# Scaling the second chunk's attention probabilities on GpSimd instead of VectorE

## The chip, the cores and the metric

The kernel runs on one core of one Trainium2 chip. The metric is the device time of one execution in microseconds (us). Beside it there is one profiled execution, whose trace holds the start and the end of every instruction on every engine: TensorE (PE, with its weight loads listed apart as PEld), VectorE (DVE), ScalarE (ACT), GpSimd (POOL) and SyncE (SP).

## The reference

The work is an attention with a sparse mask, followed by a two-layer network with a GELU. Batch 4, 8 heads, 768 positions, head size 64; each position sees a window of local keys behind it and a few global keys at the start of the sequence, with a linear bias per head:

```python
scores = scale * q @ k.T + bias                # bias = -slope[h] * distance
scores = np.where(is_global | is_local, scores, -1e9)
a = np.exp(scores - max(scores)); a = a / (sum(a) + 1e-9)
x = (a @ v)                                    # heads side by side: 3072 tokens x 512
h = x @ w_in                                   # 512 x 2048
out = 0.5 * h * (1 + erf(h / sqrt(2))) @ w_out # 2048 x 512
```

The weights arrive as 64-bit words, and the kernel rebuilds each of them as a high part and a low part so that float32 accuracy survives the matmuls.

## The kernel before

The 3072 tokens are cut into 12 chunks of 256 (c = 0 to 11). For each chunk the attention is made in four pairs of heads (p = 0 to 3), and for each pair the steps are: `scores_pair` (s, L342: 16 small matmuls; then n, L353: VectorE adds the mask penalty, writes the scores to SBUF as tile `n` and keeps their minimum), `exps` (L374: four ScalarE exponentials over 128x192 elements with their sums in `su`; L376 and L377: VectorE adds 1e-9 and takes the reciprocal; L383: four instructions multiply the four pieces of `n` by the reciprocal), `flip` once per head (t, L393: three TensorE transposes; pt, L397: ScalarE copies them to SBUF), and `av_pair` (L422: the products with v; L445 and L450: ScalarE writes the high part of `x`, L174: VectorE the low part).

A chunk's tokens then go through the network in eight steps (s = 0 to 7), one for each slice of 256 hidden columns. `m1` (h, L481 in chunks 0 and 1, L464 and L468 later) is the first product, `gelu` (L491, L492 on ScalarE, L174 gl on VectorE) the activation, and `m2` (acc, L511) the second product. Chunks 0 and 1 take their steps in turn, (0,0), (1,0), (0,1), (1,1) and so on, so that each slice of weights, once rebuilt, serves both; from chunk 2 on the chunks follow one another.

While chunks 0 and 1 run, the weights are also rebuilt, four pieces for each slice: L206 (ScalarE, low words), L212, L214 and L216 (VectorE, bit operations), L226 (ScalarE, high part), L174 winl or woutl (VectorE, low part).

The loop in `run` writes all this out step by step (T), and `START` and `EVENTS` say at which T a chunk's pair gets its scores, transposes and products: chunk 1 makes its scores at T = -3, -2, -1 and 0, and its transposes two steps later. The order in which the instructions then stand on each engine's queue is made at compile time by a scheduler with a model of their durations; it is fixed when the kernel runs, and each engine takes its instructions in that order. Some orders are forced by hand: `after` and `behind` put an instruction behind another one on its engine. `behind` uses `self.last_dve`, the last of VectorE's instructions for the attention or the network that was written out, so that a piece of weights (L212, L174) never goes ahead of it.

Of the kernel before, what the change touches and what calls it, by code (L numbers as in the profile page):

```python
# [83 lines left out]
class Fast:  # L84
# [282 lines left out]
    def exps(self, c, p):  # L367
        nc = self.nc
        first = c % CPB == 0
        mn, su = self.stat.pop((c, p))  # L370
        every = [(self.pt_n[c, 2 * p + hh][:, j * NK:j * NK + (P if first and j == 0 else NK)], 2 * hh + j)
                 for hh in range(2) for j in range(2)]
        for nn, i in every:
            self.table(nc.scalar.activation(out=nn, in_=nn, func=AF.Exp, bias=mn[:, i:i + 1],  # L374
                                            scale=-1.0, accum_out=su[:, i:i + 1]))
        nc.vector.tensor_scalar(out=su, in0=su, scalar1=1e-9, scalar2=None, op0=ALU.add)  # L376
        nc.vector.reciprocal(out=su, in_=su)  # L377
        if c >= 3:
            top = self.nmax[:, 3 * NP]
            nc.vector.tensor_tensor(out=top, in0=top, in1=mn, op=ALU.max)  # L380
        for nn, i in every:
            eng = nc.vector if c < 2 else nc.gpsimd
            ins = eng.tensor_scalar(out=nn, in0=nn, scalar1=su[:, i:i + 1], scalar2=0.0,  # L383
                                    op0=ALU.mult, op1=ALU.add)
        if c < 2:
            self.last_dve = ins.ins

    def flip(self, c, h):
# [401 lines left out]
```

## Time and profile before

| | |
|---|---|
| time before, median of 3 runs | 688.21 us (687.5 to 688.92) |
| the profiled execution: its own time | 687.72 us |
| the profiled execution: span of the core | 685.9 us |
| what lies around the span | 1.82 us |
| TensorE busy | 673.2 us, 98% of the span |
| VectorE, ScalarE, GpSimd busy | 382.3, 353.9 and 103.3 us |

The span runs from the first to the last instruction of the trace. An engine's busy time is the union of its instructions, and where an engine stood idle, the trace says which instruction of another engine ended that idle time. Times in the rows below count from the start of the span.

### The profile page before, as it was taken

The page shows a single profiled execution, that of the slowest core. Times are in us where ns is not written, and L with a number is a line of the kernel's source. Part 1 is how long each engine was busy: PE and PEld are TensorE (multiplying, and loading weights), DVE is VectorE, ACT ScalarE, POOL GpSimd, SP SyncE. Part 2 cuts the span into 40 slices and gives each one's busy share as a digit, 9 for nine tenths or more (in the row PEclk, how much of TensorE's full clock was granted, in tenths as well). Part 3 has the DMA queues.
Part 4 walks back from the last instruction along what each step waited for, and adds up shares of the span by engine and source line. Part 5 has one row for each costly group of instructions (what it writes and reads, how often), then busy time and mean ns, then how long its engine had stood idle before and what let it go on. Part 6 is the DMA issues. An engine that isn't in the chain of part 4 may idle for free.

```text
span 685.9 us, 12867 instructions
## 1 busy us (share of the span) xinstructions
PE 673.2 (98%) x4879; PEld 562.0 (82%) x4879; DVE 382.3 (56%) x1129; ACT 353.9 (52%) x846; POOL 103.3 (15%) x232
## 2 busy tenths in 40 slices
PE   8989999999999999999999999999999999999996
PEld 5668988878888888888888888888888888888785
DVE  5989998334554654644545545546445455453532
ACT  3897686554654545545527536445446365362222
POOL 3100331310200301301201111031021031010000
PEclk9999999999999999999999999999999999999999
DMA  9936933240622513403314234134053152000000
GB/s 269 285 130 193 300 131 124 78 138 33 162 62 93 162 43 113 139 19 121 99 64 155 70 94 154 33 107 131 10 162 117 38 162 62 32 1 1 33 0 35
DMA packets 66037, 71.17 MB, mean 104 GB/s; under 512 B 32688, under 2 KB 49072, under 8 KB 65968
## 3 DMA queue, kind: packets, MB, share of 16 engines
q1 hardware_dynamic: 61520, 62.80, 30.5%
q10 hardware_dynamic: 4448, 7.48, 3.1%
q8 instruction: 41, 0.67, 0.4%
q14 instruction: 28, 0.23, 0.1%
HBM read 63.97 MB, written 6.29 MB: 102 GB/s over the span
## 4 chain that ended last, share of the span: by engine, by line
PE 90%; ACT 4%; DVE 3%; issue 1%; DMA 1%; ACTq 0%; DVEq 0%; SPq 0%
PE acc L511 37%; PE h L464 22%; PE h L468 8%; PE av L422 6%; PE s L342 5%; PE h L481 4%; PE t L393 4%; PE h L470 3%; PE warm_ps L361 1%; ACT n L374 1%; ACT w L206 1%; DVE n L353 1%; DVE wb L214 1%; DVE n L383 1%; DMA w<-w 1%
## 5 line engine op out<-in xcount | busy, mean ns | idle before, releaser
L464 PE MATMUL h<-x,winh 128*128 128x512 f32 x640 | 216.0, 401 | 0.0
L472 DVE TENSOR_REDUCE hs<-h 128x256 f32<-128x512 f32 x160 | 110.3, 689 | 132.6 <-PE h L470 132.0
L511 PE MATMUL acc<-wouth,gh 128*128 128x512 f32 x384 | 157.0, 409 | 1.1 <-ACT gh L491 0.8
L511 PE MATMUL acc<-woutl,gh 128*128 128x512 f32 x384 | 150.2, 391 | 0.0
L511 PE MATMUL acc<-wouth,gl 128*128 128x512 f32 x384 | 148.5, 393 | 0.0
L383 POOL TENSOR_SCALAR n<-n,su 128x192 f32<-128x192 f32 (+1 forms) x160 | 72.6, 473 | 442.0 <-ACT n L374 225.7
L468 PE MATMUL h<-x,winl 128*128 128x256 f32 x480 | 134.7, 281 | 0.0
L464 PEld LDWEIGHTS h<-x,winh 128*128 128x128 f32 x640 | 114.3, 188 | 20.4 <-issue 0.3
L174 DVE TENSOR_TENSOR gl<-gr,gh 128x512 fp32r<-128x512 f32 x96 | 66.9, 697 | 112.5 <-ACT gr L492 112.4
L491 ACT ACTIVATE gh<-hs 128x512 fp32r<-128x512 f32 x80 | 50.7, 633 | 133.2 <-DVE hs L472 129.7
L397 ACT COPY pt<-t 128x384 f32<-128x384 f32 x96 | 45.6, 480 | 133.6 <-PE t L393 133.2
L468 PEld LDWEIGHTS h<-x,winl 128*128 128x128 f32 x480 | 90.4, 188 | 7.1
L511 PEld LDWEIGHTS acc<-wouth,gh 128*128 128x128 f32 x384 | 72.2, 188 | 19.9 <-issue 5.8
L511 PEld LDWEIGHTS acc<-wouth,gl 128*128 128x128 f32 x384 | 72.1, 188 | 16.7 <-issue 0.6
L511 PEld LDWEIGHTS acc<-woutl,gh 128*128 128x128 f32 x384 | 72.3, 188 | 12.6 <-issue 0.3
L374 ACT ACTIVATE n<-n,mn 128x192 f32<-128x192 f32 (+1 forms) x144 | 62.3, 434 | 1.7 <-DVE mn L353 1.5
L353 DVE CUSTOM_DVE_ANT_0 n<-s,pen 128x192 f32<-128x192 f32 (+1 forms) x192 | 54.9, 342 | 3.5 <-PE s L342 3.5
L481 PE MATMUL h<-x,winh 128*128 128x256 f32 x256 | 49.0, 287 | 0.4 <-ACT x L445 0.2
L492 ACT ACTIVATE gr<-hs 128x512 f32<-128x512 f32 x80 | 49.3, 616 | 0.0
L393 PE MATMUL t<-ident,n 128*128 128x128 f32 x288 | 47.2, 274 | 1.2 <-DVE n L383 1.2
L422 PE MATMUL av<-pt,vr 64*64 64x64 f32 (+1 forms) x1024 | 45.5, 246 | 2.7 <-ACT pt L397 2.6
L422 PEld LDWEIGHTS av<-pt,vr 64*64 64x64 f32 (+1 forms) x1024 | 35.1, 135 | 13.1 <-issue 5.6
(81 smaller groups left out, 729.5 us busy)
## 6 DMA issues: line engine op xcount, KB each, us to landing
w<-w SPq DMA_DIRECT2D x32, 512.0 KB, 5.3
c<-w SPq DMA_DIRECT2D x32, 512.0 KB, 5.0
out<-o ACTq DMA_DIRECT2D x24, 256.0 KB, 2.0
qr<-qT SPq DMA_DIRECT2D x11, 512.0 KB, 3.8
vr<-v SPq DMA_DIRECT2D x22, 256.0 KB, 4.1
kr<-kT SPq DMA_DIRECT2D x16, 320.0 KB, 4.9
vr<-v SPq DMA_DIRECT2D x19, 192.0 KB, 3.0
kr<-kT SPq DMA_DIRECT2D x36, 64.0 KB, 3.7
```

Of the source, the lines that this page charges most:

```text
L174: return self.nc.vector.tensor_tensor(out=out, in0=in_, in1=hi.bitcast(F32), op=ALU.subtract)
L353: ins = nc.vector.tensor_tensor_reduce(out=nn[:, j * NK:j * NK + n], in0=sp[hh][:, j, 0:n], in1=pen, scale=-slope(2 * p + hh), scalar=3e38 ...
L374: self.table(nc.scalar.activation(out=nn, in_=nn, func=AF.Exp, bias=mn[:, i:i + 1], scale=-1.0, accum_out=su[:, i:i + 1]))
L383: ins = eng.tensor_scalar(out=nn, in0=nn, scalar1=su[:, i:i + 1], scalar2=0.0, op0=ALU.mult, op1=ALU.add)
L393: nc.tensor.transpose(tp[:, i, :], nn[:, o:o + P], self.ident)
L422: ins = nc.tensor.matmul(out, lhsT=lhs, rhs=rhs, start=start, stop=stop, skip_group_check=True).ins
L464: nc.tensor.matmul(hp.rearrange("p e t -> p (e t)"), lhsT=wh[:, d, fs], rhs=x[:, d].rearrange("p e t -> p (e t)"), start=d == 0, stop=d == ...
L468: nc.tensor.matmul(hp[:, 0, :], lhsT=wl[:, d - 1, fs], rhs=x[:, d - 1, 0, :], start=False, stop=False, skip_group_check=True)
L472: self.last_dve = nc.vector.tensor_reduce(out=self.h[t][:, f, :], in_=hp.rearrange("p e t -> p t e"), axis=mybir.AxisListType.X, op=ALU.ad ...
L481: nc.tensor.matmul(hp[:, f, :], lhsT=w[:, d, fs], rhs=x[:, d, e, :], start=n == 0, stop=n == 3 * NP - 1)
L491: self.table(nc.scalar.activation(out=gh, in_=hp, func=AF.Gelu))
L511: nc.tensor.matmul(acc, lhsT=g[:, f, ks], rhs=w[:, f, :], start=s == 0 and n == 0, stop=s == NST - 1 and n == 5)
```

## The change

The multiplication of the probabilities by the reciprocal of their sum (L383) is done by VectorE for chunks 0 and 1 and by GpSimd for chunks 2 to 11. Now it is done by VectorE for chunk 0 alone. Chunk 1 has four pairs with four instructions each, so 16 instructions of 128x192 float32 change their engine. The second line of the diff goes with it: `last_dve` is no longer set to chunk 1's multiplications, so the pieces of weights that follow in the program are put behind VectorE's instruction before that.

```diff
         for nn, i in every:
-            eng = nc.vector if c < 2 else nc.gpsimd
+            eng = nc.vector if c < 1 else nc.gpsimd
             ins = eng.tensor_scalar(out=nn, in0=nn, scalar1=su[:, i:i + 1], scalar2=0.0,
                                     op0=ALU.mult, op1=ALU.add)
-        if c < 2:
+        if c < 1:
             self.last_dve = ins.ins
```

## Rows read from the trace of the kernel before

**Rows 1.** Stretches of the span: start and end in us, their length, then busy time of each engine (with its number of instructions), granted TensorE clock, DMA share, GB/s. The order of the engines is PE, PEld, DVE, ACT, POOL.

```profile
24.00:40.00 16.00, 14.17 (x140) 9.96 (x138) 15.74 (x60) 14.47 (x40) 0.00 (x0) 1.00 0.82 278
40.00:50.00 10.00, 8.22 (x86) 5.36 (x85) 8.14 (x31) 9.69 (x31) 0.00 (x0) 1.00 0.34 103
50.00:60.00 10.00, 9.10 (x93) 7.78 (x92) 9.98 (x20) 6.95 (x14) 0.00 (x0) 1.00 0.49 162
60.00:70.00 10.00, 10.00 (x66) 9.07 (x65) 10.00 (x19) 6.64 (x13) 0.00 (x0) 1.00 0.68 213
134.00:300.00 166.00, 166.00 (x1214) 140.11 (x1213) 81.75 (x252) 83.57 (x201) 25.43 (x60) 1.00 0.32 98
```

**Rows 2.** Whom TensorE waited for, over the whole span: us in total, times, longest us.

```profile
PE av L422 <- ACT pt L397: 2.6, 3, 1.3
PE t L393 <- DVE n L383: 1.2, 1, 1.2
PE acc L511 <- ACT gh L491: 0.8, 1, 0.8
```

**Rows 3.** VectorE's instructions in order of time around the multiplications of chunk 1: start us, us, engine, line, operation, tiles, shapes, count, idle time before.

```profile
29.90 0.17 DVE L377 RECIPROCAL su<-su 128x4 f32<-128x4 f32 x1
...
34.98 0.17 DVE L377 RECIPROCAL su<-su 128x4 f32<-128x4 f32 x1
...
42.28 0.18 DVE L377 RECIPROCAL su<-su 128x4 f32<-128x4 f32 x1
...
43.76 0.35 DVE L353 CUSTOM_DVE_ANT_0 n<-s,pen 128x192 f32<-128x192 f32 x1
...
44.87 0.69 DVE L174 TENSOR_TENSOR winl<-wb,winh 128x512 fp32r<-128x512 f32 x1
...
46.19 0.69 DVE L216 CUSTOM_DVE_ANT_0 wb<-w,wb 128x1024 uint16<-128x1024 uint16 x1
46.80 0.17 DVE L377 RECIPROCAL su<-su 128x4 f32<-128x4 f32 x1
47.00 1.01 DVE L383 TENSOR_SCALAR n<-n,su 128x192 f32<-128x192 f32 x4
47.92 0.42 DVE L174 TENSOR_TENSOR x<-av,x 128x256 fp32r<-128x256 f32 x1
48.26 0.76 DVE L212 TENSOR_SCALAR wb<-w 128x512 int32<-128x512 int32 x2
48.93 0.42 DVE L174 TENSOR_TENSOR x<-av,x 128x256 fp32r<-128x256 f32 x1
49.26 0.69 DVE L174 TENSOR_TENSOR winl<-wb,winh 128x512 fp32r<-128x512 f32 x1
```

**Rows 4.** TensorE's instructions in order of time: chunk 1's transposes of pairs 0, 1, 2 and 3 and what follows them; same columns.

```profile
33.37 0.82 PE L393 MATMUL t<-ident,n 128*128 128x128 f32 x6
...
37.38 0.82 PE L393 MATMUL t<-ident,n 128*128 128x128 f32 x6
...
44.04 0.55 PE L393 MATMUL t<-ident,n 128*128 128x128 f32 x3
...
45.72 0.55 PE L393 MATMUL t<-ident,n 128*128 128x128 f32 x3
47.47 0.76 PE L393 MATMUL t<-ident,n 128*128 128x128 f32 x4 [1.20 <-DVE n L383]
...
48.52 0.44 PE L393 MATMUL t<-ident,n 128*128 128x128 f32 x2
49.54 0.65 PE L422 MATMUL av<-pt,vr 128*64 128x128 f32 x6 [0.58 <-ACT pt L397]
50.12 0.51 PE L481 MATMUL h<-x,winh 128*128 128x256 f32 x2
...
53.07 0.43 PE L422 MATMUL av<-pt,vr 128*64 128x128 f32 x2
```

**Rows 5.** ScalarE's instructions in order of time before and behind pair 3's exponentials; same columns.

```profile
32.28 0.46 ACT L374 ACTIVATE n<-n,nmax 128x192 f32<-128x192 f32 x1 [0.91 <-DVE nmax L353]
...
44.15 0.46 ACT L374 ACTIVATE n<-n,nmax 128x192 f32<-128x192 f32 x1 [0.29 <-DVE nmax L353]
...
49.02 0.47 ACT L397 COPY pt<-t 128x384 f32<-128x384 f32 x1
...
49.96 0.86 ACT L397 COPY pt<-t 128x384 f32<-128x384 f32 x2
```

**Rows 6.** GpSimd's instructions in order of time, same columns, and one of VectorE's beside them.

```profile
96.34 9.24 POOL L383 TENSOR_SCALAR n<-n,su 128x192 f32<-128x192 f32 x8 [18.81 <-DVE su L377]
123.62 1.63 POOL L383 TENSOR_SCALAR n<-n,su 128x192 f32<-128x192 f32 x4 [18.04 <-DVE su L377]
...
123.65 0.35 DVE L353 CUSTOM_DVE_ANT_0 n<-s,pen 128x192 f32<-128x192 f32 x1
```

**Rows 7.** VectorE's groups of instructions: first two of the stretch 24 to 50 us, then the same two of 96 to 106 us. Shapes and count, busy us, mean ns of one, idle time before.

```profile
L216 DVE CUSTOM_DVE_ANT_0 wb<-w,wb 128x1024 uint16<-128x1024 uint16 x5 | 3.4, 688 | 0.0
L212 DVE TENSOR_SCALAR wb<-w 128x512 int32<-128x512 int32 x6 | 2.4, 421 | 0.0
...
L216 DVE CUSTOM_DVE_ANT_0 wb<-w,wb 128x1024 uint16<-128x1024 uint16 x4 | 3.1, 769 | 0.0
L212 DVE TENSOR_SCALAR wb<-w 128x512 int32<-128x512 int32 x4 | 2.0, 488 | 0.0
```

## The prediction, made before the changed kernel was run

> **What bounds the kernel now.** I read the stretches of the span first. From 60 us on TensorE is busy all the time: 10.00 of 10 us between 60 and 70, 166.00 of 166 between 134 and 300 [rows 1]. A faster or slower VectorE or GpSimd there moves nothing as long as its results come early enough. The time can only change where TensorE stands idle, and around the change that is 24 to 60 us: 14.17 of 16, 8.22 of 10 and 9.10 of 10 us busy, so 1.83 + 1.78 + 0.90 = 4.5 us idle. In the first of these stretches VectorE is busy for 15.74 of 16 us and ScalarE for 14.47; in the second ScalarE is busy for 9.69 of 10 and VectorE for 8.14. So VectorE is the fuller engine until 40 us, and ScalarE between 40 and 50.
>
> The list of TensorE's waits says what the idle time is made of [rows 2]: 2.6 us on the copies of the transposes (pt), 1.2 us on exactly the instruction that is moved (t on n L383), 0.8 us on the GELU. The 1.2 us are one wait, and the order of time places it: before the transposes at 47.47 [rows 4], which need pair 3's probabilities, multiplied from 47.00 on [rows 3]. Behind it comes another 0.58 us at 49.54, for a pt copy of pair 2 that ScalarE takes up at 49.02 [rows 4, 5]. After that the next slice's first product runs from 50.12, and pair 3's own products come only at 53.07.
>
> So the question is small and local: for four pairs, when are the probabilities ready, against when TensorE takes them.
>
> **What VectorE gets back.** The four multiplications of a pair start at 47.00 and the next instruction at 47.92 [rows 3], so they hold VectorE for 0.92 us. Four pairs make 3.7 us. That is not won from the span: behind 60 us nothing waits for VectorE, and before it only two waits shorten. ScalarE waited 0.91 us for pair 1's scores at 32.28, behind pair 0's multiplications, and 0.29 us for pair 3's at 44.15 [rows 5], behind pair 2's (VectorE starts these scores at 43.76, with a group of 0.92 us in front that goes away) [rows 3]. The 0.91 us are absorbed: pair 1's transposes stand at 37.38 [rows 4], behind a TensorE that has no wait of note until then. The 0.29 us count, since pair 3 follows directly: its reciprocal ends at 46.68 instead of 46.97.
>
> **What GpSimd takes.** The trace has no multiplication on GpSimd at this place, so I bound it from rows of the same instruction. The cheap end: four in 1.63 us at 123.62, 0.41 us each, while VectorE works on scores that it reads from PSUM [rows 6]. The dear end: eight in 9.24 us at 96.34, 1.155 us each, while VectorE rebuilds weights without a pause [rows 6]. The two engines hold each other up: in that stretch VectorE's L216 takes 769 ns and L212 takes 488, against 688 and 421 where GpSimd stands still [rows 7]. That is 0.08 and 0.07 us, and with eight of them beside eight multiplications about 0.075 us for each, so 16 x 0.075 = 1.2 us go back out of the 3.7: VectorE nets 2.5 us.
>
> The Trainium skill speaks against such a move: its page "Perfetto Trace Analysis", section "Optimizing Scalar/DVE Operations", says that the two engines share an SBUF read port, so that offloading from one to the other might not help. The rows on the two stretches agree that there is a price, nearly threefold for GpSimd; by the page alone the 3.7 us of VectorE would be no gain at all.
>
> Pair by pair, from the end of the reciprocal:
>
> Pair 0: reciprocal until 30.07, transposes at 33.37, 3.3 us for four instructions of 0.41 to 1.155 us, that is 1.6 to 4.6 us [rows 3, 4, 6]. Behind L216 and L212 VectorE makes scores there, the cheap case, so I take 2.5 us: hidden. At the dear end the second head would be 1.3 us late (30.07 + 4.62 = 34.69).
>
> Pair 1: reciprocal until 35.15, up to 0.9 us earlier by what ScalarE wins at 32.28; transposes at 37.38. Cheap end 35.9, dear end 38.9. The first head needs only two of the four, by 36.6 at the dear end. I take it as hidden; without that cover it costs up to 1.1 us.
>
> Pair 2: reciprocal until 42.46, first head's transposes at 44.04 and the second's at 45.72, while VectorE makes scores until 44.87: hidden. At the dear end its first head would be ready at 44.77, 0.7 us late, which falls into the idle 1.2 us that ends at 47.47 [rows 3, 4].
>
> Pair 3 decides. Its reciprocal ends at 46.68 with the 0.29 us. Behind it VectorE has, by its order now, an x (L174, 0.34 us, from PSUM), two L212, an x (0.33), a winl, and then more weights [rows 3]: 0.67 us of some 3.4 us are of the cheap kind, the rest of the dear one. So the first multiplication takes 0.43 us beside x and the other three 0.2 x 0.41 + 0.8 x 1.155 = 1.0 us each: 3.4 us, ready at 50.1. VectorE was ready at 47.92. The last two transposes take 0.44 us [rows 4], so they end at 50.5 instead of 48.96. The products behind them stood at 49.54 and waited for ScalarE; 0.58 us of the delay vanish in that wait, and the rest, 50.54 - 49.54 = 1.0 us, moves TensorE's work from there on. Queued behind the waiting transposes on TensorE are those products, the next slice's first product at 50.12 and pair 3's products at 53.07, and behind these ScalarE's x, the GELU and the wait of 0.8 us for it [rows 2], which therefore moves along and does not absorb it.
>
> The sum on the profiled execution: span 685.9, around it 1.82, so 687.72; plus 1.0 is 688.7. The median of the runs is 0.49 us above that execution, so I forecast 689.2 us. The bound of 0.2% (what a measurement of this kernel can tell from no change) is 1.4 us: this is still no change.
>
> **The second line of the diff** costs nothing itself. It lets a piece of weights stand ahead of the reciprocal on VectorE, for instance while VectorE waits for the exponentials. What comes of it is the order of the queues, which no row shows; it belongs to the second rival.
>
> **Rivals.** (1) Slower: the whole of pair 3 runs at the dear price, and the 0.29 us don't come. Then it is ready at 46.97 + 4.62 = 51.6, the transposes end at 52.0, and TensorE stands 2.5 us later: 690.2, as a median 690.7. For it speaks the stretch at 96 us, whose mix of instructions is what stands behind 48.26; against it the two x. It decides from the point at which four multiplications take over 3.8 us from 46.68 (50.5 + 0.44 - 49.54 = 1.4), 0.95 us each on average; my own sum is at 0.85. One way to get there: each multiplication waits out one of VectorE's long instructions, 0.61 us from start to start for L216 (46.19 to 46.80) [rows 3], and then takes its own 0.41, 1.02 us; four take 4.1, and TensorE stands 46.68 + 4.1 + 0.44 - 49.54 = 1.7 us later, 689.9 as a median. The page "SBUF — State Buffer" of the Trainium skill, section "Who interferes with whom", has this as its rule: the shared ports are an exclusive lock, and the second instruction waits until the first has ended. The dear row's 1.155 us lies above such a single wait, so the rows bear out the blocking and not its length.
>
> (2) Faster: the compile-time order changes so that TensorE has the next slice's first product in front of pair 3's transposes. They have room: pair 3's copies end at 50.8 [rows 5] and their products stand at 53.07 [rows 4], 2.2 us later. Then the waits of 1.2 and 0.58 us are filled. Against it: this product needs the slice's low part, winl, which VectorE starts at 49.26 and ends at 49.9 [rows 3], and which only moves forward with VectorE's net 2.5 us. I price it at 1.5 of the 1.8 us: 686.2, as a median 686.7.
>
> (3) Nothing to be seen: GpSimd gets through at nearly the cheap price, because VectorE has its work done earlier and pauses. Pair 3 is ready at 46.68 + 1.63 = 48.3, before the 48.52 at which its last transposes stand, and the 0.29 us remain: 687.4, as a median 687.9.
>
> **How the numbers follow.** My sum 0.38, rival 1 0.22 (0.08 of it for the single waits), rival 2 0.17, rival 3 0.23. Slower by over 0.2%: rival 1 and what my sum leaves above 1.4 us (0.06), 0.28. Faster: most of rival 2 and a remainder of orders better than it, 0.17. Within: 0.55. My own case alone reaches from 688.5 (the three behind the first at 0.75 us) to 690.0 (at 1.25); with rivals 2 and 1 the range goes from 686.6 to 690.9.
>
> **What would show it.** In the changed kernel's trace: 16 more multiplications on GpSimd between 30 and 52 us, 0.41 us each for pair 2 and about 1 us for pair 3; VectorE without L383 there; TensorE's wait for n, now on GpSimd, grown from 1.2 to over 2 us, with the last wait on pt gone; L216 and L212 longer by 0.07 to 0.08 us. The prediction is wrong if TensorE's instructions between 44 and 54 us stand in another order, if pair 0 or 1 is waited for, or if anything behind 60 us is idle that is not idle now.

## The result, and the profile after

Six runs of the changed kernel have a median of 692.96 us (691.82 to 694.48), six of the kernel before beside them 688.17 us (687.5 to 689.0). The medians lie 4.8 us apart. The ratio, by which all costs below are told, is 1.0061, with an interval from 1.0046 to 1.0075: slower by 4.2 us, where the prediction had 1 us and ended its range at 690.9.

The profiled execution took 692.18 us, its span is 690.3 us, 4.4 us longer than before. TensorE is busy for 675.0 us in it, against 673.2. So 1.8 of the 4.4 us are work that took longer, and 2.6 us are more idle time. The stretches of the changed kernel, with the columns of [rows 1]:

```profile
24.00:40.00 16.00, 14.61 (x138) 10.48 (x141) 13.97 (x52) 12.96 (x37) 5.04 (x8) 0.89 0.87 309
40.00:50.00 10.00, 6.46 (x72) 4.15 (x68) 8.29 (x24) 9.98 (x29) 4.11 (x5) 0.99 0.24 71
50.00:60.00 10.00, 8.51 (x60) 6.32 (x64) 8.52 (x16) 4.68 (x10) 3.00 (x4) 0.67 0.58 193
60.00:70.00 10.00, 9.18 (x89) 8.17 (x82) 6.19 (x13) 7.19 (x13) 0.00 (x0) 1.00 0.39 110
```

TensorE was busy for 1.76 us less between 40 and 50 us (6.46 against 8.22), for 0.59 less in the next stretch and for 0.82 less in the one behind that; the granted clock was 0.67 between 50 and 60 us, where it had been 1.00 [rows 1]. VectorE has 13.97 us of work up to 40 us where it had 15.74, so it did get its time back.

Whom TensorE waited for, as in [rows 2]:

```profile
PE t L393 <- POOL n L383: 3.9, 6, 1.0
PE av L422 <- ACT pt L397: 3.1, 3, 1.3
```

One wait of 1.2 us for VectorE has become six for GpSimd with 3.9 us in sum, and the waits for pt did not shrink. GpSimd's own order of time has only three groups there:

```profile
30.56 2.65 POOL L383 TENSOR_SCALAR n<-n,su 128x192 f32<-128x192 f32 x4 [11.06 <-DVE su L377]
34.82 2.40 POOL L383 TENSOR_SCALAR n<-n,su 128x192 f32<-128x192 f32 x4 [1.62 <-ACT w L206]
45.90 7.11 POOL L383 TENSOR_SCALAR n<-n,su 128x192 f32<-128x192 f32 x8 [8.67 <-DVE su L377]
```

Pairs 0 and 1 took 0.66 and 0.60 us for each multiplication on average; pairs 2 and 3 stand back to back, eight in 7.11 us, 0.89 us each. That pair 3 queues behind pair 2 was not foreseen; in [rows 3] their reciprocals lie 4.5 us apart. VectorE's order of time in the changed kernel shows how they came together:

```profile
43.21 0.17 DVE L376 TENSOR_SCALAR su<-su 128x4 f32<-128x4 f32 x1 [0.82 <-ACT n L374]
43.72 0.69 DVE L174 TENSOR_TENSOR winl<-wb,winh 128x512 fp32r<-128x512 f32 x1 [0.34 <-ACT winh L226]
44.33 0.69 DVE L216 CUSTOM_DVE_ANT_0 wb<-w,wb 128x1024 uint16<-128x1024 uint16 x1
44.93 0.68 DVE L214 SCALAR_TENSOR_TENSOR wb<-w,wb 128x512 int32<-128x512 int32 x1
45.53 0.17 DVE L377 RECIPROCAL su<-su 128x4 f32<-128x4 f32 x1
...
47.25 0.17 DVE L377 RECIPROCAL su<-su 128x4 f32<-128x4 f32 x1
```

Between the two short instructions that make pair 2's reciprocal (L376 at 43.21, L377 at 45.53) now stand a wait for ScalarE and three pieces of weights. From L376 to L377 it is 2.3 us. The reciprocal comes at 45.53 where it came at 42.28 [rows 3], while pair 3's came only 0.45 us later than before. And the exponentials in front were late too. ScalarE's order of time, changed kernel:

```profile
37.01 0.48 ACT L397 COPY pt<-t 128x384 f32<-128x384 f32 x1 [1.20 <-PE t L393]
37.51 1.28 ACT L491 ACT_TABLE_LOAD   x1
38.91 0.60 ACT L491 ACTIVATE gh<-h 128x512 fp32r<-128x512 f32 x1
...
41.31 0.46 ACT L374 ACTIVATE n<-n,nmax 128x192 f32<-128x192 f32 x1
```

and the same three steps in the kernel before, with no copy of pair 1 ahead of them:

```profile
36.49 1.28 ACT L491 ACT_TABLE_LOAD   x1
37.78 0.60 ACT L491 ACTIVATE gh<-h 128x512 fp32r<-128x512 f32 x1
...
40.18 0.46 ACT L374 ACTIVATE n<-n,nmax 128x192 f32<-128x192 f32 x1
```

In the changed kernel a pt copy of pair 1 stands in front of the GELU. ScalarE waits 1.20 us for its transposes, which wait for GpSimd (34.82 to 37.22), and the GELU and the exponentials of pair 2 come 1.13 us later. TensorE at the end of the chain:

```profile
46.38 0.84 PE L393 MATMUL t<-ident,n 128*128 128x128 f32 x3 [0.43 <-POOL n L383]
47.68 0.33 PE L393 MATMUL t<-ident,n 128*128 128x128 f32 x1 [0.46 <-POOL n L383]
49.03 0.44 PE L393 MATMUL t<-ident,n 128*128 128x128 f32 x2 [1.02 <-POOL n L383]
50.11 1.09 PE L393 MATMUL t<-ident,n 128*128 128x128 f32 x3 [0.65 <-POOL n L383]
...
54.73 0.80 PE L481 MATMUL h<-x,winh 128*128 128x256 f32 x2
```

Pair 2's transposes, which stood at 44.04, stand at 46.38, and the next slice's first product at 54.73 instead of 50.12 [rows 4], in an order that is not that of before: the transposes of pair 2 and pair 3 now follow one another without other work between them, where before products stood between the two heads of pair 2. The clock in the middle of it, stretches of 2 us:

```profile
48.00:50.00 2.00, 0.44 (x3) 0.20 (x2) 2.00 (x5) 2.00 (x7) 2.00 (x2) 0.96 0.38 123
50.00:52.00 2.00, 1.11 (x4) 0.50 (x4) 2.00 (x5) 1.62 (x5) 2.00 (x4) 0.50 0.74 281
54.00:56.00 2.00, 2.00 (x14) 1.67 (x11) 1.33 (x4) 1.93 (x4) 0.00 (x0) 0.50 0.50 199
```

Behind the stretch with 0.44 us of work in 2 the granted clock is 0.50, the lower of the two levels, 1.2 GHz. It stays there until some way into the stretch behind 56 us, while TensorE is busy again for all of its time from 54 us on. This is where work takes longer: its matmuls with winl take 0.41 us there and 0.28 us later.

### The profile page after: what moved, and what is told of

Same layout as the page of the kernel before. It is cut to its first block, busy times and chain, and to the rows that moved or that the text cites. A ratio compares the mean times of both kernels' runs of the same rounds, so it can differ in the third digit from the quotient of the medians.

```text
span 690.3 us, 12873 instructions
## 1 busy us (share of the span) xinstructions
PE 675.0 (98%) x4879; PEld 563.6 (82%) x4879; DVE 379.4 (55%) x1113; ACT 354.8 (51%) x846; POOL 124.5 (18%) x248
## 4 chain that ended last, share of the span: by engine, by line
PE 94%; ACT 2%; DVE 2%; POOL 1%; issue 1%; ACTq 0%; POOLq 0%; DVEq 0%
PE acc L511 38%; PE h L464 22%; PE h L468 8%; PE h L481 7%; PE av L422 6%; PE s L342 5%; PE t L393 4%; PE h L470 3%; PE warm_ps L361 1%; ACT n L374 1%; POOL n L383 1%; DVE n L353 0%; ACT o L517 0%; DVE wb L214 0%; DVE n L383 0%
## 5 line engine op out<-in xcount | busy, mean ns | idle before, releaser
L383 POOL TENSOR_SCALAR n<-n,su 128x192 f32<-128x192 f32 (+1 forms) x176 | 80.9, 478 | 455.6 <-ACT n L374 247.1
L393 PE MATMUL t<-ident,n 128*128 128x128 f32 x288 | 49.3, 279 | 4.1 <-POOL n L383 3.9
L422 PE MATMUL av<-pt,vr 64*64 64x64 f32 (+1 forms) x1024 | 45.3, 247 | 3.1 <-ACT pt L397 3.1
L422 PEld LDWEIGHTS av<-pt,vr 64*64 64x64 f32 (+1 forms) x1024 | 35.3, 135 | 13.1 <-issue 5.6
```

What stands on the lines that cost most here:

```text
L393: nc.tensor.transpose(tp[:, i, :], nn[:, o:o + P], self.ident)
L422: ins = nc.tensor.matmul(out, lhsT=lhs, rhs=rhs, start=start, stop=stop, skip_group_check=True).ins
```

## The experiments

The theory after this reading: the cost does not come from GpSimd's multiplications, it comes from the order that the scheduler made at compile time when they were given to another engine. The rival: GpSimd is slow beside VectorE's weight work, and the waits for it would come in any order. First each line of the diff alone.

**The second line alone.** VectorE keeps all multiplications:

```diff
-        if c < 2:
+        if c < 1:
             self.last_dve = ins.ins
```

> Only the second line of the change: chunk 1's multiplications stay on VectorE, and last_dve is no longer set to them. Theory order: the weight pieces ahead of the reciprocal cost time on VectorE too, 690 us or more. Theory speed: no change, 688.2 within 1.4 us.

Measured: 692.47 us beside 688.80, ratio 1.0046 [1.0028, 1.0064], as theory order had it. TensorE's waits show one line that matters, and VectorE's order of time its cause:

```profile
PE t L393 <- DVE n L383: 4.9, 1, 4.9
```

```profile
47.75 0.16 DVE L376 TENSOR_SCALAR su<-su 128x4 f32<-128x4 f32 x1
...
49.36 0.17 DVE L377 RECIPROCAL su<-su 128x4 f32<-128x4 f32 x1
...
50.96 1.00 DVE L383 TENSOR_SCALAR n<-n,su 128x192 f32<-128x192 f32 x4
```

Pair 3's L376, L377 and L383 have weights and pieces of x between them: 3.2 us from the start of the first to the start of the last. In the kernel before, it is 0.93 us, with one piece of weights in between (46.19) and L383 at 47.00 [rows 3]:

```profile
46.07 0.16 DVE L376 TENSOR_SCALAR su<-su 128x4 f32<-128x4 f32 x1
```

So a line that changes no instruction costs 3.2 us here by the ratio (3.7 between the medians), without GpSimd.

**The first line alone.** GpSimd multiplies, but weights are still kept behind chunk 1's attention, now behind its reciprocal:

```diff
-        nc.vector.reciprocal(out=su, in_=su)
+        rec = nc.vector.reciprocal(out=su, in_=su)
...
-            eng = nc.vector if c < 2 else nc.gpsimd
+            eng = nc.vector if c < 1 else nc.gpsimd
...
         if c < 2:
-            self.last_dve = ins.ins
+            self.last_dve = ins.ins if c < 1 else rec.ins
```

> Chunk 1's multiplications on GpSimd as in the change, but last_dve is set to VectorE's reciprocal of the pair, so that later pieces of weights stay behind it. Theory order (the loss comes from pair 2's reciprocal, which stands behind three weight instructions in the changed kernel, 2.3 us late, so that pairs 2 and 3 queue up together on GpSimd): most of the 4.8 us goes, 688 to 690 us, and TensorE's wait for GpSimd falls from 3.9 us to under 1.5. Theory speed (the loss comes from GpSimd's 0.9 us for each multiplication beside VectorE's weight work): 691 us or more, with a wait of over 3 us left.

Measured: 695.41 us, ratio 1.0088 [1.0070, 1.0107], no better than both lines together. That is what theory speed had said, and theory order's 688 to 690 us was missed. But the order changed again, so it isn't the test that was meant. ScalarE has both copies of pair 1 in front of the GELU, each waiting for transposes:

```profile
36.50 0.48 ACT L397 COPY pt<-t 128x384 f32<-128x384 f32 x1 [0.91 <-PE t L393]
37.77 0.48 ACT L397 COPY pt<-t 128x384 f32<-128x384 f32 x1 [0.80 <-PE t L393]
...
39.56 0.60 ACT L491 ACTIVATE gh<-h 128x512 fp32r<-128x512 f32 x1
```

The waits for GpSimd sum to 4.5 us. This alone can't tell order from speed.

**Only pairs 0 and 1 on GpSimd**, the two that the prediction called hidden; the weights stay behind VectorE's last attention instruction of each pair:

```diff
+            eng = nc.vector if c < 1 or (c == 1 and p > 1) else nc.gpsimd
```

> Only pairs 0 and 1 of chunk 1 on GpSimd (last_dve set to their reciprocals), pairs 2 and 3 on VectorE. Both theories put the loss at pairs 2 and 3: 687 to 689.6 us. If pairs 0 and 1 cost something themselves (the wait of 1.20 us of ScalarE for pair 1's transposes at 37 us in the changed kernel speaks for it), 690 us or more.

Measured: 696.03 us, ratio 1.0101 [1.0075, 1.0128], the slowest of all, far above the 687 to 689.6 us that both theories gave. TensorE's wait for GpSimd is a single one of 0.3 us. Its largest wait is for VectorE:

```profile
PE t L393 <- DVE n L383: 3.8, 1, 3.8
```

VectorE has eight multiplications fewer, TensorE next to no wait for GpSimd, and the time is 7 us longer. This speaks against the rival, but the order is still another one. To settle it, the order has to be held.

**GpSimd in the order of before.** The instructions carry the same names in both kernels. So the order in which TensorE, VectorE, ScalarE and SyncE have them in one kernel, as far as some 135 us, can be written down and forced on the other, with the same `after` that the kernel uses:

```python
def pin(fast):
    made = {i.name: i for i in fast.nc.all_instructions()}
    for order in ORDER:            # one list of names for each engine, of the kernel before
        seq = [made[f"I-{n}"] for n in order if f"I-{n}" in made]
        for prev, ins in zip(seq, seq[1:]):
            fast.after(ins, prev, "the order of the other kernel")
```

Here the changed kernel gets the order of before; the 16 multiplications leave VectorE's queue and nothing else moves. In the trace, TensorE, ScalarE and VectorE (without L383) have their instructions in exactly the order of the kernel before, over the whole span.

> The 16 multiplications run on GpSimd as in the changed kernel, but TensorE, VectorE, ScalarE and SyncE keep, instruction for instruction, the order of the kernel before; the 16 instructions are only taken out of VectorE's queue. Theory A (the order made at compile time carries most of the cost, GpSimd's own slowness about what the prediction's sum gave it): pairs 0 and 1 are not waited for, pair 3's transposes wait 1.5 to 2.5 us for GpSimd instead of 1.2 us for VectorE, and the time is 688.3 to 690.2 us, a ratio of 1.000 to 1.003 to the kernel before. Theory B (GpSimd's speed beside VectorE's weight work carries it, whatever the order): TensorE's waits for n sum to over 3.5 us here too, the clock falls behind them, and the time is 692 us or more, a ratio of 1.0055 or more.

Measured: 689.69 us (11 runs) beside 688.78 (21 runs), ratio 1.0011 [0.9998, 1.0024]. Theory A holds. GpSimd's order of time:

```profile
30.09 2.19 POOL L383 TENSOR_SCALAR n<-n,su 128x192 f32<-128x192 f32 x4 [9.60 <-ACT pt L397]
35.32 2.75 POOL L383 TENSOR_SCALAR n<-n,su 128x192 f32<-128x192 f32 x4 [3.05 <-DVE su L377]
43.14 1.63 POOL L383 TENSOR_SCALAR n<-n,su 128x192 f32<-128x192 f32 x4 [5.08 <-ACT w L206]
47.17 2.58 POOL L383 TENSOR_SCALAR n<-n,su 128x192 f32<-128x192 f32 x4 [2.40 <-ACT pt L397]
```

and TensorE's at pair 3:

```profile
47.65 0.84 PE L393 MATMUL t<-ident,n 128*128 128x128 f32 x3 [1.21 <-POOL n L383]
48.87 0.33 PE L393 MATMUL t<-ident,n 128*128 128x128 f32 x1 [0.38 <-POOL n L383]
...
49.80 0.49 PE L393 MATMUL t<-ident,n 128*128 128x128 f32 x2 [0.24 <-POOL n L383]
50.22 1.11 PE L422 MATMUL av<-pt,vr 128*64 128x128 f32 x6
51.26 0.80 PE L481 MATMUL h<-x,winh 128*128 128x256 f32 x2
```

Pairs 0, 1 and 2 are not waited for. Pair 3 is, three times, 1.8 us in sum. The products behind its transposes (L422) stand 0.68 us later than in [rows 4], and the next slice's first product 1.14 us later: the six products take 1.04 us from start to start where they took 0.58, and the granted clock is 0.52 there.

```profile
50.00:52.00 2.00, 2.00 (x11) 1.45 (x11) 2.00 (x5) 1.03 (x4) 0.00 (x0) 0.52 0.00 0
```

The span of this execution is 687.9 us, 2.0 us longer than before, and TensorE is busy for 675.5 us in it, against 673.2. So TensorE is idle for 12.4 us, no longer than the 12.7 us of the kernel before, and all of the 2.0 us is work that took longer. (The profiled execution of the kernel before, 687.72 us, is one of its quicker ones; between the medians it is 0.9 us.)

**VectorE in the order of the changed kernel.** The counterpart: the order of the changed kernel is forced on VectorE's version, with each pair's four multiplications directly behind its reciprocal.

> VectorE makes all 16 multiplications, four directly behind each pair's reciprocal, and everything else on TensorE, VectorE, ScalarE and SyncE stands in the order of the changed kernel. Theory A (order): pair 1's copy still goes ahead of the GELU, pair 2's reciprocal still stands behind three pieces of weights and is about 2.3 us later than before, and VectorE has its 3.7 us of multiplications on top: 690.5 to 692.5 us, a ratio of 1.003 to 1.006. Theory B (GpSimd's speed): with multiplications of 0.23 us instead of 0.6 to 0.9 us each the waits for n fall to 1.5 us or less, and the time is 688 to 689.5 us, a ratio under 1.002.

Measured: 695.29 us (5 runs), ratio 1.0079 [1.0048, 1.0109]. That is above both ranges: theory B is out, and theory A's size was too low. TensorE's waits for n do fall to 1.4 us, as theory B said, and the time does not fall with them. VectorE's order of time shows that fast multiplications don't help when they start late:

```profile
44.77 0.17 DVE L376 TENSOR_SCALAR su<-su 128x4 f32<-128x4 f32 x1 [0.92 <-ACT n L374]
...
47.10 0.17 DVE L377 RECIPROCAL su<-su 128x4 f32<-128x4 f32 x1
47.30 1.01 DVE L383 TENSOR_SCALAR n<-n,su 128x192 f32<-128x192 f32 x4
```

The 2.3 us between L376 and L377 are the same as in the changed kernel, and all of it is 1.6 us later (44.77 against 43.21). With its multiplications VectorE is busy for 15.59 of the 16 us before 40, TensorE waits for an x that VectorE makes (2.8 us in two waits), which it does nowhere in the changed kernel, and the GELU waits 1.19 us for a product of TensorE. So this run shows that the order is a bad one without GpSimd too, but part of its 5.4 us comes from VectorE's fuller queue. In this order the move to GpSimd is, if anything, a help: the two intervals overlap.

**Pairs 0, 1 and 2 on GpSimd, pair 3 on VectorE, order of before.** It takes away the only wait that the run in the order of before had left.

> Order of the kernel before on all other engines; the multiplications of pairs 0, 1 and 2 run on GpSimd, those of pair 3 on VectorE as before. It tests the prediction's word that pairs 0, 1 and 2 are hidden as long as the order stays. Theory A: no wait of TensorE for GpSimd above 0.3 us, the wait for pair 3 on VectorE is 0.9 to 1.2 us, and the time is 687.5 to 688.8 us, a ratio of 0.998 to 1.001. Theory B: the first transposes of pairs 0 to 2 wait for GpSimd by over 1 us in sum, and the time is 690 us or more, a ratio of 1.003 or more.

Measured: 688.22 us (11 runs), ratio 0.9993 [0.9979, 1.0008]. Theory A holds: TensorE has no wait for GpSimd of note, and

```profile
PE t L393 <- DVE n L383: 0.9, 1, 0.9
```

is what remains of the wait of 1.2 us in [rows 2], 0.3 us less. It is the best version found and does not measurably beat the kernel before. It also shows that forcing this order by itself costs nothing that can be seen. Beside the run with pairs 0 and 1 (ratio 1.0101) it moves one pair more to GpSimd, so GpSimd can't explain the difference of 1%; what is left is the order.

**Which part of the order.** The order can be cut in two: up to pair 1's transposes and copies and the first gl, and from there on. GpSimd multiplies in all of these. First the start as in the changed kernel and the rest as before:

> The other half: the queues stand in the order of the changed kernel as far as that point, so that pair 1's transposes and its first copy go ahead of the GELU and two pieces of weights ahead of pair 0's reciprocal, and from there on in the order of the kernel before, with the reciprocals of pairs 2 and 3 directly behind their exponentials or one piece of weights. Theory P: the exponentials of pair 2 start about 1.1 us later than before, and all behind them, and the time is 691 to 693 us, a ratio of 1.0035 to 1.006. Theory Q: the 1.1 us remain beside the 1.0 us of pair 3 on GpSimd, without the later waits, and the time is 689.5 to 690.8 us, a ratio of 1.001 to 1.003.

Measured: 691.32 us (7 runs) beside 688.68, ratio 1.0033 [1.0020, 1.0047], at the lower end of theory P's times, with a ratio between the two. ScalarE has the copy in front of the GELU again, and pair 2's exponentials stand at 41.67, where they stand at 40.67 in the order of before:

```profile
37.36 0.48 ACT L397 COPY pt<-t 128x384 f32<-128x384 f32 x1 [1.20 <-PE t L393]
...
41.67 0.46 ACT L374 ACTIVATE n<-n,nmax 128x192 f32<-128x192 f32 x1
```

Over the whole order of before (1.0011) this half adds 0.22%, 1.5 us, but the two intervals overlap, and in the profile TensorE is idle no longer than there (12.4 us in both). That this half alone costs something over the order of before is not shown. Now the other half:

> GpSimd makes the 16 multiplications. The queues of TensorE, VectorE and ScalarE stand in the order of the kernel before until chunk 0's first gl (VectorE), pair 1's two pt copies behind pair 2's exponentials (ScalarE) and the end of pair 1's transposes (TensorE); from there on in the order of the changed kernel. So pair 1's copy is no longer ahead of the GELU, but pair 2's reciprocal still stands behind pieces of weights, with pair 3's behind it. Theory P (the order around pair 1 carries the cost, since everything behind the GELU moves with it): the rest of the order costs under 1 us, and the time is 689.5 to 690.5 us, a ratio of 1.001 to 1.0025. Theory Q (the late reciprocals of pairs 2 and 3 carry it): pair 2's reciprocal still comes over 1.5 us behind its exponentials, TensorE's waits for n sum to over 3 us, and the time is 691 to 693 us, a ratio of 1.0035 to 1.006.

Measured: 695.32 us, ratio 1.0090 [1.0068, 1.0113]. It tells nothing on either theory: by the cut, a product of pair 1 stood ahead of pair 3's scores on TensorE while its copy stood late on ScalarE, and TensorE waited for it once for 4.0 us, which it does in neither kernel. With that one product put back:

> As the run with the start in the order of before and the rest in that of the changed kernel, but one product of pair 1 on TensorE stays behind the second product of the network, where the kernel before has it; in the other run it stood ahead of pair 3's scores while its pt copy stood late on ScalarE, and TensorE waited 4.0 us for that copy, a wait that neither kernel has. If the costs of the two halves of the order add up (1.0011 for GpSimd in the order before, 1.0033 with the first half of the new order, 1.0061 with both), this half alone gives 1.0039, 691.0 to 692.0 us beside 688.7, with pair 2's reciprocal more than 1.5 us behind its exponentials and pair 3's multiplications directly behind pair 2's on GpSimd. If the second half costs something only because the first has made it late, the time is 689.5 to 690.5 us.

Measured: 692.31 us (10 runs) beside 689.32, ratio 1.0047 [1.0034, 1.0060]. VectorE and GpSimd in order of time:

```profile
41.61 0.17 DVE L376 TENSOR_SCALAR su<-su 128x4 f32<-128x4 f32 x1
...
45.19 0.17 DVE L377 RECIPROCAL su<-su 128x4 f32<-128x4 f32 x1
```

```profile
45.55 7.07 POOL L383 TENSOR_SCALAR n<-n,su 128x192 f32<-128x192 f32 x8 [7.98 <-DVE su L377]
```

Pair 2's exponentials are in time, its reciprocal is 3.6 us behind L376 all the same (the piece winl in between waits 1.60 us for ScalarE), and pairs 2 and 3 are back to back as in the changed kernel. The time lies a little above the 691.0 to 692.0 us expected; the ratio of 1.0039 expected lies inside the interval. This half adds 0.36% over 1.0011, clear of the interval there, so the second half is not merely a consequence of the first. With the first half it adds to 0.11 + 0.22 + 0.36 = 0.69%, and the changed kernel has 0.61 [0.46, 0.75]: the halves agree with a plain sum, as far as these intervals can tell.

**The clock.** In the changed kernel, four matmuls of zeros, 128x384, are put ahead of the transposes of each head of pairs 2 and 3, into the same bank, where TensorE would stand idle:

```diff
+        tp = self.bank([P, 3, P], f"t{c}_{h}"); self.warm(4 if c == 1 and h > 3 else 0, ..., out=tp...)
```

> The changed kernel with four idle-time matmuls of zeros (128x384) in front of the transposes of each of the four heads of pairs 2 and 3, into the bank that the transposes then overwrite; about 0.8 us for each head, which lies in TensorE's wait for GpSimd. Theory clock (1.8 of the 4.4 us of span are TensorE's matmuls at the lower granted clock from 50 to 56.5 us, after the stretch of waits): the granted clock stays at 1.00 there and the time falls to 690.5 to 691.5 us, although nothing else is made faster. Without it: 692.5 to 693.5 us.

Measured: 692.25 us (690.27 to 693.55, 7 runs), ratio 1.0035 [1.0014, 1.0056]. The median lies between the two ranges and decides for neither. The two runs with the highest mean granted clock, 0.999, took 690.27 and 690.64 us; the two with 0.993 and 0.994 took 693.55 and 692.52. In the profiled one (693.03 us) the clock still falls, only later:

```profile
54.00:56.00 2.00, 1.75 (x14) 1.41 (x15) 1.05 (x3) 1.27 (x3) 0.20 (x1) 0.85 0.72 221
56.00:58.00 2.00, 2.00 (x12) 2.00 (x10) 2.00 (x5) 0.89 (x2) 0.00 (x0) 0.50 0.16 64
```

So about 0.26% may be the clock, 1.8 us like the longer work in the profile, but this interval overlaps that of the changed kernel, and behind 50 us the order of this run is another one again. Nor is the clock this change's alone: of the 21 runs of the kernel before that stood beside the runs with forced order, four have a mean of 0.992 and took 689.6 to 690.9 us, those of 0.997 and above 686.9 to 689.6. In the six runs of the changed kernel it is 0.988 to 0.992 every time. Its four runs at 0.991 and 0.992 took 691.8 to 694.5 us, so at about the same clock some 2.6 us are left between the medians of these four and those four (they did not run beside one another), as much as the idle time in the profile had grown.

## Why the prediction was wrong

**The step that failed** is "The second line of the diff costs nothing itself", and with it the assumption under the whole sum, that the queues keep their order. The prediction named the order as unknown and then priced it only as a gain (rival 2, 686.7 us). The runs show it as a loss: with the order held the change costs 0.8 us (1.0011), with the order that the scheduler made 4.2 us (1.0061). So some 3.4 us of it, 0.50% (1.0061 less 1.0011), come with the order, and the second line alone, in which no multiplication changes its engine, costs 3.2 us (1.0046). In the profiled executions the order's part is idle time of TensorE: 15.3 us in the changed kernel, 12.4 us with the order held and 12.7 us before.

**The sum came out near for the order of before, and in part by luck.** It said 1.0 us, and the run with that order gave 0.8, with an interval from -0.1 to 1.7. What held: pairs 0, 1 and 2 are hidden, and pair 2 has the cheap price, 0.41 us (1.63 us for four). The last wait on pt did go, as foretold (2.6 us to 2.0). That VectorE's net gain does not move the end also holds: with pair 3 left on VectorE the time is within 0.2%. What was mis-sized is pair 3: predicted 3.4 us for four, one at 0.43 and three at 1.0, measured 2.58, with 0.43, 0.43, 0.84 and 0.95. The products behind it, for which the sum has its 1.0 us, stand 0.68 us later. And the profile of that run shows no idle time added, only work that took longer. Over the runs it is the same: at a mean clock of 0.997 three runs of this version took 688.3 to 688.7 us, and ten of the kernel before 687.8 to 689.6. So the 0.8 us may be the clock alone, which was in no term, and its nearness to 1.0 is luck.

**Pair 1 as hidden** held only in the order of before, where its transposes stand at 37.38, behind products of the network [rows 4]. In the changed kernel they start at 36.08, ahead of those products, while GpSimd multiplies until 37.22, and a copy of them stands ahead of the GELU, which comes 1.13 us later. This does not show as a wait of TensorE for pair 1 but as a wait of ScalarE, 1.20 us, so the test "if pair 0 or 1 is waited for" looked at the wrong engine. The prediction's "up to 1.1 us" was a price for TensorE waiting; no row ties the GELU's delay to it, so that the two have the same size proves nothing.

**Pair 2 as hidden** failed by a delay that no rival had: not GpSimd's four multiplications but the reciprocal in front of them, 2.3 us behind L376 with weights in between, on top of the 1.13 us of the exponentials. That also brought pair 3 in behind pair 2 on GpSimd, at 0.89 us each on average beside VectorE's weights: near the 0.85 that the sum had as its mean for pair 3, for eight instead of four.

**The clock** was in no term. The prediction moved TensorE's work by the length of a wait and let it run at full speed afterwards. Here 1.8 of 4.4 us are work that takes longer, and with the order held all of the 2.0 us.

**The test that was written down held**: "The prediction is wrong if TensorE's instructions between 44 and 54 us stand in another order". They do. Why the scheduler now puts more weights between a pair's L376 and L377 (one piece stands there for pair 3 in the kernel before, none for pair 2) was not tried; no run shows its reasons, and the second line alone is enough for it.

## What to carry to other kernels

Where the order is made at compile time, moving an instruction to another engine, or an order edge that costs nothing, makes a new order for everything around it; compare the instruction sequences of all engines before reading durations, and give the new order a price on both sides when predicting. To learn what the engine itself costs, force the old order on the new code; here that split 4.2 us into 0.8 and 3.4 in one run. When VectorE only prepares a short scalar for a longer step elsewhere (here L376 and L377, 0.17 us each), the place of that pair in its queue can be worth more than the step's own speed, as it was here. And before a small difference is put down to a wait, the idle time and the busy time of the two profiles have to be told apart, since longer work at a lower clock made 2 us in one profile here.

## What the runs showed of the hardware

GpSimd's multiplication of 128x192 has no single price. The means of groups are 0.41 us while VectorE reads scores from PSUM (pair 2 in the order of before), 0.55 to 0.81 for the other pairs with forced orders, 0.89 in eight behind each other beside weights, 1.11 for pair 3 in the run with the first line alone (4.45 us for four), near the 1.155 of [rows 6]. These means mix two kinds: in the changed kernel pair 1's four took 1.20, 0.42, 0.42 and 0.42 us, and the eight of pairs 2 and 3 range from 0.42 to 1.49. One instruction is held up and the next is not. VectorE's L216 paid for it, with 0.789 us on average between 45 and 54 us of the changed kernel against 0.688 in [rows 7], 0.10 us more where 0.08 was expected, while L212 took 0.408 and paid nothing, against the 0.07 us expected. The Trainium skill has the two engines exclude each other on the port that they share (page "SBUF — State Buffer", section "Who interferes with whom"); by a wait for the whole of one L216 the prediction had 1.02 us for each. That both engines lose time agrees with the page; that a multiplication loses nothing in one place and up to 1.07 us in another (1.49 against 0.42) is what the rows add.

The granted clock of the changed kernel went to its lower level behind a run of short waits, 0.4 to 1.0 us each with work between them, and stayed there for some seven microseconds, the last two or three of them with TensorE busy all the time. A drop of this kind between 30 and 34 us is in the profile of the changed kernel too and not in that of before. But of two kernels with the same order up to there, that with all 16 multiplications on GpSimd has it (0.89 between 24 and 40 us) and that with 12 does not (1.00), and the run with the second line alone, which has none of the 16 on GpSimd, has it (0.89). What decides there stays open.
